# Two more groups of 256 tokens leave the attention rounds of a fused attention and MLP-mixer kernel for its late part

## The chip, the cores and the metric

The kernel runs on one core of a Trainium2 chip. The metric is the time of one execution on the device, in microseconds (us). The time is that of three runs: median, lowest and highest. Beside it stands one profiled execution, recorded by the hardware profiler, whose span runs from the first to the last instruction of the program. The engines are TensorE (PE in the profile, with its weight loads as PEld), VectorE (DVE), ScalarE (ACT), GpSimd (POOL) and SyncE (SP), which here only issues DMA transfers. A "q" behind an engine's name is the queue that issues its DMAs.

## What is computed

```python
# q, k, v: (8, 8, 576, 64) float32: batch, heads, tokens, head size
scores = (q @ k.transpose(0, 1, 3, 2)) / 8.0
thresh = scores.max(-1, keepdims=True) - tau            # tau = 0.02
scores = np.where(scores >= thresh, scores, -1e9)
attn = np.exp(scores - scores.max(-1, keepdims=True))
attn = attn / (attn.sum(-1, keepdims=True) + 1e-9)
x = (attn @ v).transpose(0, 2, 1, 3).reshape(8, 576, 512)

# w_tok1 (576, 256), w_tok2 (256, 576), w_ch1 (512, 1536), w_ch2 (1536, 512)
xt = x.transpose(0, 2, 1)
u = x + (np.maximum(xt @ w_tok1, 0) @ w_tok2).transpose(0, 2, 1)   # token MLP
out = u + np.maximum(u @ w_ch1, 0) @ w_ch2                         # channel MLP
```

Everything is float32; the MLP weights come as 64-bit numbers and are brought to float32 on the chip. A batch row has 576 tokens of 512 channels. The token MLP mixes all tokens of a row, so it can start when a row's attention is done. The channel MLP treats each token by itself, so it may be done for any group of tokens at any time after that.

## The kernel before, in words

**Attention.** The eight rows (here: batch entries, `b`) are worked one after the other. Two heads form a pair, two pairs a block of 1152 query rows, cut into nine units of 128. Two units are a *round*: 72 rounds in all, nine to a row, numbered here from 0, so that row 6 is rounds 54 to 62. A round's scores are products of TensorE (line 729) into a PSUM tile of its own pool. VectorE takes the maxima (742), GpSimd makes a bias of them (747), ScalarE masks (757) and exponentiates (767), VectorE inverts the sums (272, 273), GpSimd scales (280). Then the unit is turned: in row 0 by TensorE (295), in later rows by a VectorE transpose of 32 x 32 blocks (310) and four DMAs issued by SyncE (322, in the helper `move`). Three turned units make a group for the value products (360, 365), whose result is copied to `xT` (369), the row's activations with channels on partitions. There are two `xT` buffers, so row b + 2 writes the one that row b was in.

**Token MLP.** When a row's values are out, its token MLP follows: transposes (394), first layer (406), second layer (418), and an addition into `xT` by VectorE (428), so that `xT` now holds u.

**Channel MLP, now or late.** Of the 576 tokens of a row, `NOW[b]` groups of 256 (`GR`) get their channel MLP "now", by plain products placed between the rounds of the following rows: 12 steps of the first layer (834) with a relu each (ScalarE 839 or VectorE 842), and eight of the second layer (850), each added to the turned u by VectorE (864) and stored (874). The turn of u takes two VectorE transposes (819) and eight DMAs (826). In row 0 a group adds u by an identity product (848) instead and needs no turn. The tokens that are not done now are spilled to DRAM by one DMA a row (`spill`, 470). Row 7 has no groups now, and none of it is spilled.

**The late part.** After the last round the attention's memory is released and the remaining tokens are done in units of 512 (class `Late`): a channel MLP by Strassen's scheme with seven products of half-size blocks instead of eight, all on TensorE at line 1192. Its weight sums (`w1s`, `w2s`) are made by six VectorE operations, and sums of u (`t`) by four for each unit, at lines 1113 and 1116. The units are built from the list `put_off`, two groups of 256 each, and one more unit of the last 64 tokens of all rows. A unit's u is loaded from the spills (1147).

**What sets the order.** A planner written out in the kernel (class `Scheduler`) simulates the engines with given costs and emits instructions in the order that it finds; on the chip each engine then works strictly through its own list. All steps of TensorE outside the scores draw on banks of PSUM: two until the last round, four after it. Ranks decide between steps that are ready: value products 0, scores 1, token MLP 1.5, channel MLP 2. Besides, a round's scores are held back until the filling that has been done by the planner's count (`self.done`) has reached a due amount:

```python
total = sum(TOKENS + NOW[r] * GROUP for r in range(row))
part = TOKENS + NOW[row] * GROUP if row < B - 1 else 0.0
return total + part * (k - 2) / (UB // 2) - (KEEP_LAST if row == B - 2 else KEEP)
```

Here `row` is the row before the one whose rounds are placed, `k` the round in its row, `TOKENS` 18.8, `GROUP` 41.8, `KEEP` 14 and `KEEP_LAST` 20, in the planner's microseconds. A row's value products wait for the last reads of the `xT` two rows before it, the first layer of that row's groups and its spill among them.

Of the kernel before, what the change touches and what calls it, by code (L numbers as in the profile page):

```python
# [21 lines left out]
def kernel(  # L22
# [26 lines left out]
    B, H, S, D = q.shape  # L49
# [410 lines left out]
        return steps  # L460


    NOW = [2] + [1] * (B - 2) + [0]
    spilled = {}

    def spill(b):

        lo = GR * NOW[b]
        spilled[b] = dram.tile([P, NCC, S - lo], F32, name=f"spill_{b}")
# [335 lines left out]
    def make_groups(b, halves):  # L805
        uT = xTs[b]
        reads = []
        for i in range(NOW[b]):
            s = {}
# [240 lines left out]
    def planned_at(row, k):  # L1050
# [4 lines that stand above are left out]
# [72 lines left out]
    REST = S - 2 * GR  # L1127
    put_off = [(b, GR * i, GR) for b in range(B) for i in range(NOW[b], 2)]
    groups = [put_off[i : i + 2] for i in range(0, len(put_off), 2)]
    assert all(len(g) == 2 for g in groups) and not NOW[B - 1]  # L1130
    groups.append([(b, 2 * GR, REST) for b in range(B)])
# [239 lines left out]
```

## Time and profile before

| | us |
|---|---|
| median of three runs (lowest, highest) | 1346.2 (1345.57, 1347.57) |
| the profiled execution | 1346.21 |
| its span | 1344.3 |
| last round's scores begin | 895.7 |
| late part's first product begins | 976.5 |
| TensorE busy | 1261.7 |
| VectorE busy | 802.1 |
| ScalarE busy | 570.9 |

The profiled execution is 1.9 us longer than its span. A table of stretches is read so: first the stretch in us from the start of the span and its length, then for each engine the busy time and in brackets the number of instructions, then the clock that TensorE was granted (1.00 is full), the mean busy share of the 16 DMA engines and the rate at which they moved data. In a list of waits, three numbers stand behind a pair: us in total, how often, the longest. In a timeline the two leading numbers are the start and the length. A float32 product is recorded as two matmuls, so the first layer of a group has 96 records and the second 192.

### The profile page before, as it was taken

The page shows a single profiled execution, that of the slowest core. Times are in us where ns is not written, and L with a number is a line of the kernel's source. Part 1 is how long each engine was busy: PE and PEld are TensorE (multiplying, and loading weights), DVE is VectorE, ACT ScalarE, POOL GpSimd, SP SyncE. Part 2 cuts the span into 40 slices and gives each one's busy share as a digit, 9 for nine tenths or more (in the row PEclk, how much of TensorE's full clock was granted, in tenths as well). Part 3 has the DMA queues.
Part 4 walks back from the last instruction along what each step waited for, and adds up shares of the span by engine and source line. Part 5 has one row for each costly group of instructions (what it writes and reads, how often), then busy time and mean ns, then how long its engine had stood idle before and what let it go on. Part 6 is the DMA issues. An engine that isn't in the chain of part 4 may idle for free.

```text
span 1344.3 us, 21936 instructions
## 1 busy us (share of the span) xinstructions
PE 1261.7 (94%) x7982; PEld 1002.0 (75%) x7982; DVE 802.1 (60%) x1449; ACT 570.9 (42%) x1244; POOL 354.2 (26%) x658
## 2 busy tenths in 40 slices
PE   6778899999989999998999999899999999999998
PEld 5555579688657866875785776687988888888887
DVE  7899965384756766586576667665154443444352
ACT  6888654464644554455355537541020211112020
POOL 4666522142423323333233323320000000010100
PEclk7798899999989999999999999999999999999999
DMA  9655673463776575675667477173020211021011
GB/s 175 153 137 153 145 166 85 88 153 87 180 168 141 125 161 137 140 155 128 143 157 156 118 154 164 49 180 90 9 69 18 64 32 32 24 58 30 32 32 32
DMA packets 307194, 145.11 MB, mean 108 GB/s; under 512 B 206672, under 2 KB 299856, under 8 KB 307088
## 3 DMA queue, kind: packets, MB, share of 16 engines
q1 hardware_dynamic: 305216, 143.51, 46.3%
q8 instruction: 63, 1.03, 0.3%
q10 hardware_dynamic: 1872, 0.21, 0.1%
q14 instruction: 43, 0.35, 0.1%
HBM read 47.32 MB, written 13.50 MB: 45 GB/s over the span
## 4 chain that ended last, share of the span: by engine, by line
PE 58%; DVE 16%; SPq 10%; ACT 6%; DMA 6%; issue 3%; POOL 1%; DVEq 0%; ACTq 0%; POOLq 0%
PE o L1192 10%; PE bank L850 8%; PE bank L834 7%; SPq L322 6%; DVE mx L742 6%; PE hx L1192 6%; PE bank L365 5%; PE sc L729 5%; PE hz L1192 4%; PE oz L1192 4%; PE hmm L1192 4%; DVE T L310 3%; ACT e L757 3%; ACT e L767 2%; DMA eT<-T 2%
## 5 line engine op out<-in xcount | busy, mean ns | idle before, releaser
L757 ACT ACTIVATE e<-sc,bias 128x576 f32<-128x576 f32 x288 | 197.5, 741 | 223.6 <-DVE mx L742 180.8
L280 POOL TENSOR_SCALAR e<-e,rr 128x576 f32<-128x576 f32 x288 | 211.9, 750 | 284.9 <-DVE rr L273 239.1
L742 DVE TENSOR_REDUCE mx<-sc 128x1 f32<-128x576 f32 x288 | 198.1, 744 | 44.1 <-PE sc L729 44.1
L767 ACT ACTIVATE e<-e,ntau 128x576 f32<-128x576 f32 x288 | 221.0, 779 | 0.2
L310 DVE STREAM_TRANSPOSE T<-e 128x1152 f32<-128x1152 f32 x126 | 171.7, 1369 | 54.4 <-DMA eT<-T 42.3
L729 PE MATMUL sc<-kT,qT 64*128 64x192 f32 (+1 forms) x1920 | 176.4, 345 | 15.8 <-ACT e L757 13.6
L729 PEld LDWEIGHTS sc<-kT,qT 64*128 64x128 f32 (+1 forms) x1920 | 145.7, 183 | 47.9 <-issue 20.3
L850 PEld LDWEIGHTS bank<-wc,g 128*128 128x128 f32 x1536 | 175.0, 192 | 8.5 <-issue 4.9
L850 PE MATMUL bank<-wc,g 128*128 128x128 f32 x1536 | 180.0, 277 | 0.1
L834 PE MATMUL bank<-xT,wc 128*128 128x256 f32 x768 | 177.5, 384 | 0.9 <-DVE g L842 0.7
L834 PEld LDWEIGHTS bank<-xT,wc 128*128 128x128 f32 x768 | 142.4, 190 | 32.6 <-issue 7.5
L365 PE MATMUL bank<-eT,lv 128*64 128x384 f32 (+1 forms) x1024 | 146.5, 431 | 0.0
L747 POOL TENSOR_SCALAR bias<-mx,toff 128x1 f32<-128x1 f32 x288 | 77.7, 273 | 251.2 <-DVE mx L742 249.9
L1275 POOL TENSOR_TENSOR us<-us,ut 128x256 f32<-128x256 f32 x27 | 22.4, 844 | 393.2 <-DVE us L1113 393.2
L365 PEld LDWEIGHTS bank<-eT,lv 128*64 128x64 f32 x1024 | 81.8, 145 | 54.9 <-issue 38.6
L418 PE MATMUL bank<-w,a 128*128 128x288 f32 x256 | 72.4, 426 | 19.9 <-DVE xT L428 18.7
L272 DVE TENSOR_SCALAR rr<-rs 128x2 f32<-128x2 f32 x144 | 42.4, 294 | 68.0 <-ACT e L767 67.5
L418 PEld LDWEIGHTS bank<-w,a 128*128 128x128 f32 x256 | 47.0, 193 | 40.6 <-DVE xT L428 24.5
L406 PE MATMUL bank<-x_sb,w 128*128 128x512 f32 (+1 forms) x180 | 71.3, 549 | 0.6 <-DVE x_sb L398 0.5
L360 PE MATMUL bank<-eT,vl 128*64 128x384 f32 (+1 forms) x256 | 46.9, 444 | 20.1 <-DMA lq<-in_q_dram 3.8
L1240 ACT ACTIVATE ga<-hmm 128x256 f32<-128x256 f32 x30 | 11.5, 384 | 117.1 <-PE hmm L1192 117.1
L1113 DVE TENSOR_TENSOR temps<-hx,temps 128x256 f32<-128x256 f32 x60 | 25.1, 419 | 56.7 <-PE hx L1192 56.6
(128 smaller groups left out, 1552.4 us busy)
## 6 DMA issues: line engine op xcount, KB each, us to landing
eT<-T SPq DMA_DIRECT2D x504, 144.0 KB, 3.0
lk<-in_k_dram SPq DMA_DIRECT2D x126, 72.0 KB, 3.1
lq<-in_q_dram SPq DMA_DIRECT2D x124, 72.0 KB, 3.2
out_dram<-us SPq DMA_DIRECT2D x32, 256.0 KB, 2.1
ut<-us SPq DMA_DIRECT2D x128, 64.0 KB, 2.1
lv<-in_v_dram SPq DMA_DIRECT2D x112, 72.0 KB, 2.5
spare<-in_moe_w_ch_dram SPq DMA_DIRECT2D x8, 512.0 KB, 3.9
extra<-in_moe_w_ch_dram SPq DMA_DIRECT2D x8, 512.0 KB, 3.7
```

The source lines that it names most:

```text
L280: nc.gpsimd.tensor_scalar(out=eh, in0=eh, scalar1=rr[:, h : h + 1], scalar2=1.0, op0=ALU.mult, op1=ALU.mult)
L310: nc.vector.transpose(out=T.rearrange("p a (c x) -> p c a x", c=NK), in_=e.rearrange("p (c a x) -> p c a x", c=NK, a=4))
L322: nc.sync.dma_start(out=turned_e[key][:, place, i, :], in_=T[32 * i : 32 * i + 32])
L365: nc.tensor.matmul(to[r], lhsT=lv[:, j, :], rhs=e[j], start=False, stop=(c == NI - 1), skip_group_check=True)
L418: nc.tensor.matmul(bank[:, 0:HS], lhsT=hidden[b][:, m, P * c : P * c + P], rhs=w2[:, m, HS * f : HS * f + HS], start=(m == 0), stop=(m == ...
L729: nc.tensor.matmul(sc[h][rows, f, HT * k : HT * k + HT], lhsT=qT[r, cols], rhs=kT[r, HT * f : HT * f + HT], start=True, stop=True, skip_gr ...
L742: nc.vector.tensor_reduce(out=mx[:, h : h + 1], in_=part[h], axis=AX.XY, op=ALU.max)
L757: nc.scalar.activation(out=eh, in_=part[h], func=AF.Prelu, bias=bias[:, h : h + 1], scale=SCALE, alpha=STEEP)
L767: nc.scalar.activation(out=eh, in_=eh, func=AF.Exp, bias=ntau, accum_out=rs[:, h : h + 1])
L834: nc.tensor.matmul(bank[:, 0:n], lhsT=wc1[:, j, c, :], rhs=uT[:, c, GR * i : GR * i + n], start=(c == 0), stop=(c == NCC - 1))
L850: nc.tensor.matmul(to, lhsT=s["g"][:, j, P * t : P * t + P], rhs=wc2[:, j, P * c : P * c + P], start=(j == 0 and b > 0), stop=(j == NJ - 1 ...
L1192: nc.tensor.matmul(ps, lhsT=l, rhs=r, start=start and x == 0, stop=x == len(pairs) - 1, skip_group_check=not start)
```

## The change

One line of the kernel is different: the number of groups of each row that are done between rounds.

```diff
-    NOW = [2] + [1] * (B - 2) + [0]
+    NOW = [1, 1, 1, 1, 1, 0, 1, 0]
```

Before, the list is 2, 1, 1, 1, 1, 1, 1, 0: eight groups now. After, it has six: row 0 does one instead of two, row 5 none instead of one. The two groups go to `put_off`, which grows from eight groups to ten, and so from four late units of 512 tokens to five; the unit of the last 64 tokens of all rows stays. Row 0 spills 320 tokens instead of 64, row 5 all 576 instead of 320. The due amounts of the rounds follow `NOW`: rounds of row 1 count 60.6 of the planner's microseconds for row 0 instead of 102.4, and rounds of row 6 count 18.8 for row 5 instead of 60.6. The planner runs anew with all this, so that the order of instructions is different on every engine from round 14 on.

## The prediction

> **What bounds the kernel now.** I read the page first, then a table of busy time by stretches, cut where the rows of attention begin, then TensorE's waits, then its timeline.
>
> ```profile
> span 1344.3 us, 21936 instructions
> ...
> PE 1261.7 (94%) x7982; PEld 1002.0 (75%) x7982; DVE 802.1 (60%) x1449; ACT 570.9 (42%) x1244; POOL 354.2 (26%) x658
> ...
> PE 58%; DVE 16%; SPq 10%; ACT 6%; DMA 6%; issue 3%; POOL 1%; DVEq 0%; ACTq 0%; POOLq 0%
> ```
>
> TensorE (PE) is the busiest by far and leads the chain that ended last, but that chain also passes VectorE and the DMA issues of SyncE: the mean hides stages. The stretches, in order: the second half of row 1 (rounds 14 to 17), rows 2 to 7, the rest of the attention stage, and one late unit of 512 tokens.
>
> ```profile
> core 0: us, PE busy (x) PEld busy (x) DVE busy (x) ACT busy (x) POOL busy (x), PEclk, DMA share, GB/s
> 173.00:252.20 79.20, 78.61 (x566) 64.57 (x564) 33.76 (x60) 34.10 (x80) 18.84 (x36) 1.00 0.56 122
> 252.20:350.40 98.20, 95.69 (x689) 74.19 (x688) 64.04 (x112) 53.73 (x120) 32.87 (x68) 1.00 0.52 119
> 350.40:467.70 117.30, 107.65 (x785) 80.20 (x784) 75.83 (x138) 60.76 (x134) 35.80 (x72) 0.97 0.66 147
> 467.70:579.50 111.80, 105.08 (x754) 78.50 (x752) 74.07 (x135) 58.11 (x125) 36.06 (x73) 0.98 0.65 148
> 579.50:686.10 106.60, 100.83 (x714) 76.85 (x712) 70.80 (x131) 53.82 (x118) 35.38 (x72) 0.98 0.62 140
> 686.10:801.60 115.50, 107.84 (x785) 81.08 (x784) 77.76 (x143) 58.91 (x128) 37.95 (x75) 0.97 0.66 149
> 801.60:895.70 94.10, 88.06 (x602) 64.38 (x600) 63.53 (x114) 51.81 (x112) 32.53 (x66) 1.00 0.55 130
> 895.70:976.50 80.80, 80.80 (x542) 68.54 (x541) 29.23 (x44) 14.93 (x33) 3.99 (x8) 1.00 0.22 61
> 1049.00:1121.60 72.60, 72.60 (x338) 63.92 (x337) 31.33 (x58) 10.89 (x26) 4.91 (x6) 1.00 0.15 44
> ```
>
> The reader is to see that TensorE is never idle in the last two stretches, and idle 2 to 10 us in each row from 2 to 7; from row 1's second half to the last round that is 722.7 us elapsed less 683.8 busy, so 38.9 us. No other engine is above 68% there. So a microsecond of matmul taken out of the rows is a microsecond gained, as long as the rounds that are left still have enough matmuls to fill them. What idles TensorE in a row is seen in its waits and in one round:
>
> ```profile
> PE bank L418 <- DVE xT L428: 18.7, 12, 2.6
> PE sc L729 <- ACT e L757: 13.6, 6, 5.3
> ```
>
> ```profile
> 408.91 2.22 PE L729 MATMUL sc<-kT,qT 64*128 64x192 f32 x24
> 411.06 2.21 PE L418 MATMUL bank<-w,a 128*128 128x288 f32 x8
> 414.44 2.21 PE L418 MATMUL bank<-w,a 128*128 128x288 f32 x8 [1.18 <-DVE xT L428]
> 416.58 0.60 PE L729 MATMUL sc<-kT,qT 64*128 64x192 f32 x4
> ```
>
> Round 31 has nothing to offer TensorE between its scores and the next but a few products of the token MLP. These use the two PSUM banks that all filling shares, and VectorE, in its own order, empties them too late. Attention then sets the pace: from one score to the next 7.7 us, for 6.8 us of matmuls. I call a round lean if its matmuls are under 9.5 us.
>
> **The change part by part.** *What leaves the rows.* Two groups of 256 tokens: row 0's second and row 5's only one. Busy time of the first layer's line over row 0's second group, and of first and second layer over row 5's group:
>
> ```profile
> 204.60:320.80 116.20, 22.13 (x97) 17.75 (x96) 1.00 0.45 100
> ...
> 803.70:912.20 108.50, 22.11 (x96) 17.95 (x97) 1.00 0.55 131
> 803.70:912.20 108.50, 22.27 (x192) 21.69 (x192) 1.00 0.55 131
> ```
>
> Row 5: 22.1 + 22.3 = 44.4 us. Row 0: 22.1, half of the 44.73 us that line 850 has for both its groups, and half of 4.59 us for the identity products of line 848: 46.8. Together 91.2, the upper end. Where TensorE never stops, 56 first-layer records took 12.09 us (so 96 take 20.7) and 192 second-layer ones 21.44: two groups are 84.3, the lower end. Pricing each round of both programs by such durations (scores 2.25 or 3.4 us, 20 value records 3.0, a whole token MLP 21, and the rates above), the rounds 14 to 70 hold 706 us before and 639 after, and what follows the last round 85 and 66: 86.3 less. I take 87.5. Their relus, evacuations, the turn of row 5's tokens (two transposes of 1.13 us, eight DMA issues of 0.60 us on SyncE) and four stores go too, from engines and a queue with room, for nothing.
>
> *What comes.* A fifth late unit of 512 tokens with Strassen's seven products: 336 records, 72.5 us, as each of the four there (1013.1 to 1085.6 between like instructions). TensorE has no gap in them and VectorE, the next, is 31 us busy: +72.5 (to 72.6). Its load and stores ride on SyncE at a DMA share of 0.15.
>
> *What is less well filled.* By the order of instructions, rows 2 to 5 keep their filling (431 us after, 422 before), only shifted. Row 1's second half falls from 81 to 44 us, row 6 from 112 to 85, row 7 from 91 to 79. Before, 22 rounds from 14 to 70 are lean: 181 us of matmuls, 201.3 elapsed, so 9.15 us each. After, 23 are: 186 us, at 9.15 each 210.5, so 24.5 us of slack against 20.4: +4.0. Lower end: only what falls below 8.0 us, about the fastest lean round, is lost (8.4 against 6.5): +1.9. Upper: the seven lean rounds of rows 6 and 7 before took 9.4 each (7.5 us of slack); eight at that pace with 60.7 us of matmuls have 14.8: +7.3.
>
> *Rounds 14 to 17* were idle for 0.6 us in 79; at the 6 to 8% of rows 3 to 6, 44 us idle 3. They still have only first- and second-layer products and values to mix, and no tokens: +1 (0 to 3).
>
> *Spills.* Row 5 spills 1152 KB instead of 640, row 0 640 instead of 128. 640 KB landed in 4.1 us, 128 in 2.3, so each lands 1.8 us later. Queued behind them on SyncE are moves of turned scores (line 322), for which VectorE and the value products wait: +0.5 (0 to 3.6).
>
> *Clock.* Between 355 and 381 us TensorE was 20.84 us busy, with one wait of 3.83, and its granted clock was 0.87, so about 2.7 us were lost; in round 31, with a wait of 1.18, it was 1.00. A lean round is not paced by matmuls, so most of it is hidden: +0.5 (0 to 4, from one and a half such stretches).
>
> The Trainium skill ("TensorE: Matmul & The Clock Gate", Why this matters for your kernels) says that an idle gap beyond about 3 us between bursts sends the clock back to half. The 3.83 us wait with its 0.87 agrees. It speaks against this change, which thins the matmuls: were each of the eight lean rounds of rows 6 and 7 to lose half of a window of 3.4 us that the page states, an estimate from it is 8 x 1.7 = 13.6 us, and the sum would end near the time before. By the row I keep 0.5, since the longest of the twelve waits of line 418 is 2.6 us.
>
> *Row 7's values.* The xT buffers are two, so a row's first value product waits for the first-layer products two rows back; in rows 4 to 7 before, two value groups come at once after the last of these (rounds 40, 50, 59, 69). Row 5 has none after the change, and row 7's come in rounds 65 to 70 one or two at a time: -0.5 (-6, its whole idle time, to 0).
>
> *The end of the attention stage.* Before, six sums for the late part (10.5 us of VectorE, from 917.9 us) ran while 58 us of matmuls were left, and no evacuation stood among them. After, about 40 us are left there, second-layer products between the steps of row 7's tokens, and three of their evacuations stand on VectorE among the sums and the four that turn u into t, the first behind four sums, 7.0 us. After the attention stage there are four banks, not two, so TensorE can run ahead: +1 (0 to 7).
>
> *Sum.* -87.5 + 72.5 + 4.0 + 1 + 0.5 + 0.5 - 0.5 + 1 = -8.5 us. The profiled execution took 1346.21 us, span 1344.3 and 1.9 around it, and stands at the median of the three (1346.2). So 1337.7 us. All lower ends: 1323; all upper ends: 1359.
>
> **The rivals.**
> *More gain.* The matmuls were worth their busy time (-91.2) and row 7 loses its idle time (-6): 1346.2 - 8.5 - 3.7 - 5.5 = 1328.5. For it: row 7 becomes the smoothest row. Against: its idle time before has the token phase in it, which stays.
>
> *Nothing measurable.* VectorE's sums hold up the evacuations at the end (7, not 1) and row 1 takes its 3: 1337.7 + 8 = 1345.7. For it: VectorE works in its order, and a late transfer of u would hold all behind it. Against: four banks, and no wait at all there before.
>
> *Slower.* The rounds of rows 6 and 7 fall to the pace of the DMAs and of VectorE's order, in one place: the eight lean ones (54, 57, 58, 62, 64, 67, 68, 70). In each round SyncE issues eight moves and about five loads at 0.6 us, 8 us in all, and each round has 7.6 us of VectorE for attention alone (four maxima of 0.74, two transposes of 1.37, and smaller ones). The worst such round before:
>
> ```profile
> 613.00:625.00 12.00, 9.39 (x46) 6.59 (x44) 7.31 (x13) 6.25 (x13) 3.94 (x8) 0.86 0.88 206
> ```
>
> Here 7.9 us of work took 12 us, at a DMA share of 0.88. Eight at 12.0 instead of 9.15 are +22.8: 1360.5. It decides from 10.2 us a round, where the 8.5 are used up. Against it: most lean rounds took 7.5 to 10.
>
> That the change does not do what it says is excluded: the changed order has six groups in the rows and 2016 late matmul records instead of 1680.
>
> **How the numbers follow.** The forecast has 0.57, more gain 0.13, nothing measurable 0.12, slower 0.18. What this kernel's times can tell from no change is 0.2%, 2.7 us. Faster is 0.70, within 0.12, slower 0.18. The forecast's own range is 1331 to 1343; with the rivals 1328 to 1351, which leaves out the far half of the slower case and a little below.
>
> **What would show it.** Right: late matmuls begin near 895 us instead of 976.5, five units of 72.5 us follow, and TensorE's idle time from round 14 to the first late matmul is near 45 us instead of 39. Row 6 should take 90 us or less, row 7 near 85, their lean rounds about 9. Wrong: lean rounds of rows 6 and 7 above 10.2, a granted clock under 0.95 there, or a wait of TensorE on the second layer's evacuation after the last round.

## The result, and the profile after

The changed kernel takes 1341.5 us (median of 22 executions, 1335.5 to 1348.3) and the kernel before 1345.5 us (median of 22, 1341.2 to 1352.6) on the same chip. The ratio is 0.9970, with a 95% interval of 0.9956 to 0.9984: faster by 0.3%, about 4 us, where 8.5 us were forecast. On another chip the same two kernels stood at 1340.1 (12 executions) and 1342.0 (29): 0.9986, from 0.9971 to 1.0001. So the gain is real on the first chip, small, and at the edge of what can be told on the second.

The page of the changed kernel, the lines that answer to those shown of before:

```profile
span 1336.7 us, 21554 instructions
...
PE 1243.7 (93%) x7734; PEld 984.8 (74%) x7734; DVE 824.5 (62%) x1492; ACT 573.1 (43%) x1243; POOL 359.8 (27%) x664
...
PE 61%; DVE 13%; SPq 11%; DMA 7%; ACT 5%; issue 3%; POOL 1%; DVEq 0%; ACTq 0%; POOLq 0%
```

The stretches, cut at the same rounds as before: rounds 14 to 17, rows 2 to 7, the rest of the attention stage, and one late unit. Columns are start and end, length, busy time and instructions of each engine, granted clock, DMA share and rate.

```profile
173.40:219.50 46.10, 42.40 (x303) 33.04 (x301) 31.34 (x58) 26.23 (x59) 18.16 (x36) 1.00 0.81 177
219.50:317.00 97.50, 91.30 (x665) 68.29 (x663) 65.96 (x116) 56.88 (x125) 33.77 (x69) 0.98 0.61 140
317.00:430.70 113.70, 103.32 (x753) 78.97 (x752) 75.86 (x138) 57.12 (x124) 35.86 (x72) 1.00 0.65 147
430.70:540.00 109.30, 104.90 (x785) 79.40 (x784) 75.94 (x141) 58.91 (x128) 36.46 (x73) 1.00 0.67 150
540.00:661.80 121.80, 114.17 (x794) 87.00 (x792) 76.20 (x134) 60.23 (x132) 38.41 (x76) 0.97 0.63 144
661.80:747.80 86.00, 80.86 (x609) 59.54 (x608) 62.54 (x115) 54.62 (x115) 32.78 (x68) 1.00 0.70 158
747.80:835.00 87.20, 76.37 (x538) 51.65 (x536) 63.25 (x114) 49.41 (x107) 31.69 (x64) 0.96 0.66 156
835.00:896.50 61.50, 61.50 (x405) 50.20 (x405) 29.22 (x44) 14.20 (x33) 6.86 (x12) 1.00 0.27 70
...
896.50:969.00 72.50, 72.50 (x338) 63.65 (x337) 34.38 (x60) 10.88 (x26) 4.18 (x5) 1.00 0.15 44
```

The late part begins at 896.6 us instead of 976.5 and is one unit of 72.5 us longer. Rows 2 to 5 take about as long as before (442.3 us against 433.9), row 6 is down from 115.5 to 86.0, row 7 from 94.1 to 87.2, rounds 14 to 17 from 79.2 to 46.1. TensorE (the first busy column) is idle for 3.7 us in rounds 14 to 17 where it was 0.6, and for 10.8 in row 7 where it was 6.0.

A second profile of each kernel was taken (the first two experiments below, on two other chips), so the stages can be set beside each other twice, first pair and second pair, in us:

| | before | after | difference |
|---|---|---|---|
| up to round 14 | 173.1 / 174.1 | 173.5 / 172.4 | +0.4 / -1.7 |
| rounds 14 to 70, TensorE busy | 683.7 / 680.1 | 613.3 / 615.5 | -70.4 / -64.6 |
| rounds 14 to 70, TensorE idle | 38.9 / 38.6 | 48.3 / 47.3 | +9.4 / +8.7 |
| from the last round to the late part | 80.8 / 80.8 | 61.5 / 61.5 | -19.3 / -19.3 |
| late part | 362.9 / 362.9 | 435.4 / 435.4 | +72.5 / +72.5 |
| sum | | | -7.4 / -4.4 |

The spans differ by 7.6 and by 4.6 us; the rest lies behind the last product. So of the matmul time that the change saves, 17.2 us in the first pair and 11.4 in the second, some 9 go to rounds that TensorE no longer fills. Which executions are compared matters as much: the two pairs differ by 3 us, and both profiles of the changed kernel are of executions faster than its medians (1338.65 and 1338.69 us against 1341.5 and 1340.1).

### The profile page after: what moved, and what is told of

The parts are those of the page before. It is cut to its first block, busy times and chain, and to the rows that moved or that the text cites. A ratio compares the mean times of both kernels' runs of the same rounds, so it can differ in the third digit from the quotient of the medians.

```text
span 1336.7 us, 21554 instructions
## 1 busy us (share of the span) xinstructions
PE 1243.7 (93%) x7734; PEld 984.8 (74%) x7734; DVE 824.5 (62%) x1492; ACT 573.1 (43%) x1243; POOL 359.8 (27%) x664
## 3 DMA queue, kind: packets, MB, share of 16 engines
q1 hardware_dynamic: 307040, 146.13, 47.3%
## 4 chain that ended last, share of the span: by engine, by line
PE 61%; DVE 13%; SPq 11%; DMA 7%; ACT 5%; issue 3%; POOL 1%; DVEq 0%; ACTq 0%; POOLq 0%
PE o L1192 12%; PE hx L1192 7%; SPq L322 7%; PE sc L729 6%; PE bank L365 5%; DVE mx L742 5%; PE bank L850 5%; PE bank L834 5%; PE hz L1192 5%; PE oz L1192 5%; PE hmm L1192 5%; PE bank L418 2%; DVE T L310 2%; DMA eT<-T 2%; DMA lv<-in_v_dram 2%
## 5 line engine op out<-in xcount | busy, mean ns | idle before, releaser
L1275 POOL TENSOR_TENSOR us<-us,ut 128x256 f32<-128x256 f32 x33 | 27.3, 843 | 440.3 <-DVE us L1113 440.3
L365 PE MATMUL bank<-eT,lv 128*64 128x384 f32 (+1 forms) x1024 | 140.2, 416 | 0.0
L850 PEld LDWEIGHTS bank<-wc,g 128*128 128x128 f32 x1152 | 131.7, 192 | 7.2 <-issue 4.9
L850 PE MATMUL bank<-wc,g 128*128 128x128 f32 x1152 | 135.9, 277 | 0.1
L834 PE MATMUL bank<-xT,wc 128*128 128x256 f32 x576 | 134.5, 385 | 0.4 <-ACT x_sb L398 0.2
L834 PEld LDWEIGHTS bank<-xT,wc 128*128 128x128 f32 x576 | 106.4, 190 | 25.5 <-issue 5.4
L418 PE MATMUL bank<-w,a 128*128 128x288 f32 x256 | 75.1, 439 | 23.8 <-DVE xT L428 21.5
L272 DVE TENSOR_SCALAR rr<-rs 128x2 f32<-128x2 f32 x144 | 40.3, 280 | 61.2 <-ACT e L767 60.6
L1113 DVE TENSOR_TENSOR temps<-hx,temps 128x256 f32<-128x256 f32 x72 | 30.3, 421 | 68.4 <-PE hx L1192 68.3
```

The costliest lines, as they stand in the source:

```text
L365: nc.tensor.matmul(to[r], lhsT=lv[:, j, :], rhs=e[j], start=False, stop=(c == NI - 1), skip_group_check=True)
L418: nc.tensor.matmul(bank[:, 0:HS], lhsT=hidden[b][:, m, P * c : P * c + P], rhs=w2[:, m, HS * f : HS * f + HS], start=(m == 0), stop=(m == ...
L834: nc.tensor.matmul(bank[:, 0:n], lhsT=wc1[:, j, c, :], rhs=uT[:, c, GR * i : GR * i + n], start=(c == 0), stop=(c == NCC - 1))
L850: nc.tensor.matmul(to, lhsT=s["g"][:, j, P * t : P * t + P], rhs=wc2[:, j, P * c : P * c + P], start=(j == 0 and b > 0), stop=(j == NJ - 1 ...
```

## The experiments

The forecast rests on this theory, called A in most expectations: a stage lasts as long as its matmuls, except where a round has fewer of them than attention's own pace; what is lost there is slack. Its rivals: only the number of groups counts (D); TensorE bounds every round (B), or the other engines pace them all (R); and for the missing part of the gain, executions that differ among themselves.

**The same two kernels again.** First the changed kernel, with no edit.

> The changed kernel once more, unaltered. In its first profile the sum came out as worked out: rounds 14 to 70 took 61.1 us less than before, what follows the last round 19.3 less, the late part 72.6 more, 7.8 us in all; but the medians of many executions are only 4.0 us apart. Theory A (the executions of one kernel differ in the attention stage, by its waits and TensorE's granted clock, and the first profiles were a lucky pair): the second profile shows the late part at 72.5 us a unit and the end stage at 61 to 62 us as before, and rounds 14 to 70 longer than 661.6 us by about 3, with a clock of 0.97 or less. Theory B (the gain of the stages is real and 7.8): the second profile again has 661 to 662 us there, and the medians in this run are 7 to 8 apart.

Measured: 1340.1 us against 1342.0 before. The second profile has 662.8 us in rounds 14 to 70 and a clock of 0.975, nearly the first one's. So the changed kernel's first profile was no outlier among its profiles; but the medians are 1.9 apart, not 7 or 8, so this expectation's B falls too. That left the profile of before, taken again, also unaltered.

> The kernel before once more, for a second profile. The first had 722.6 us from round 14 to the last round, 38.9 of them idle for TensorE, and a granted clock of 0.975 over the span; other executions of this kernel have a mean clock of 0.977. Theory A (the first profile of before was a slow draw, and so the gain of 7.6 us between the first profiles is too large): the second has a higher clock, a shorter stage, 717 to 720 us, with the end stage and the late part unchanged at 80.8 and 362.9. Theory B (it was typical): 722 to 723 again.

Measured: span 1341.5, rounds 14 to 70 in 718.7 us, clock 0.976. Theory A of this run holds: the first profile of before was about 3 us slower than the second. The difference lies in matmuls that took longer at a lower clock, not in waits: idle time is 38.9 and 38.6, busy time 683.7 and 680.1. The same stretch of 115.5 us, row 6 in the first profile and some 3 us more than row 6 in the second, holds 785 matmul records at a granted clock of 0.97 and 805 at 0.99:

```profile
686.10:801.60 115.50, 107.84 (x785) 81.08 (x784) 77.76 (x143) 58.91 (x128) 37.95 (x75) 0.97 0.66 149
```

```profile
686.10:801.60 115.50, 108.94 (x805) 83.09 (x802) 80.09 (x146) 58.26 (x127) 39.02 (x76) 0.99 0.67 152
```

In the first profile two short stretches of this row have half the clock. TensorE had just waited 2.0 us in front of the one and 2.3 us in front of the other:

```profile
706.10:709.30 3.20, 3.20 (x12) 1.49 (x10) 0.42 (x1) 3.20 (x8) 0.26 (x1) 0.50 0.87 220
781.20:784.40 3.20, 3.20 (x12) 1.50 (x10) 0.00 (x0) 3.20 (x9) 0.00 (x0) 0.50 0.93 234
```

The second profile has one such stretch in row 6. In rounds 14 to 70 the clock is at half for 20 us in the first profile and for 14 in the second.

**Which rows give up their groups.** Six groups again, with row 6's put off instead of row 5's:

```diff
-    NOW = [1, 1, 1, 1, 1, 0, 1, 0]
+    NOW = [1, 1, 1, 1, 1, 1, 0, 0]
```

> Six groups between the rounds as in the change, but row 6 gives up its group and row 5 keeps it. Pricing the rounds by the order of instructions: rounds 9 to 70 hold 23 us more matmuls than in the change, what follows the last round 23 us less, and the slack of lean rounds is 3.5 us smaller. Theory A (which row gives up its group matters only through slack and the end): 1338 us, the same as the change within 4. Theory C (the end stage needs filling that covers the six weight sums on VectorE, 10.5 us, and the token steps of row 7): the end stage has only 43 us of matmuls and shows 8 to 14 us of idle TensorE, 1346 to 1352.

Measured: 1339.4 us, ratio to before 0.9978 (0.9963 to 0.9994), within 1 us of the changed kernel on that chip. The end stage, now 44.1 us, has 3.4 us of idle TensorE, not 8 to 14: the weight sums need little cover, and C falls. Then both groups from row 0:

```diff
-    NOW = [1, 1, 1, 1, 1, 0, 1, 0]
+    NOW = [0, 1, 1, 1, 1, 1, 1, 0]
```

> Both of row 0's groups wait for the late part, row 5 keeps its group: again six groups. Rounds 14 to 17 have hardly any filling. Theory A (a group taken from rounds that stay filled is gained, one taken from rounds that fall under the pace of attention, about 8.6 us a round, is lost in slack): the slack of lean rounds is 38 us instead of 20, matmuls of the attention stage are the same within 2 us: 17 us slower than the change, 1357. Theory D (what counts is only the number of groups and Strassen's saving): 1340, the same as the change within 4.

Measured: 1346.4 us, ratio 1.0025 (1.0009 to 1.0042): slower than before, and 6 us slower than the changed kernel. That is between A and D: idle time of TensorE in rounds 14 to 70 is 52.7 us, only 4.4 over the changed kernel's; rounds 14 to 17 and row 2 have 16 us more of it, later rows less. The direction is A's, the size a third of it. In the profiles 7 us more come from matmuls that are longer busy (681.9 against 674.8 us from round 14 to the late part), which A does not have. And four groups:

```diff
-    NOW = [1, 1, 1, 1, 1, 0, 1, 0]
+    NOW = [1, 0, 1, 0, 1, 0, 1, 0]
```

> Four groups between the rounds (rows 0, 2, 4 and 6), four more than before in the late part, which gets a sixth unit of 512 tokens. Theory A: matmuls fall by another 85 us and the late part grows by 72.5, but slack of lean rounds grows from 20 to 46 us: 14 us slower than the change, 1354. Theory D (each pair of groups saves what the first saved): 1337 or less. The floor of a round, 8.6 us in this sum, is read from the rounds without filling.

Measured: 1359.6 us, ratio 1.0135 (1.0107 to 1.0162). D falls: the second pair costs 19 us where the first gained 2 to 4. A's 1354 is 5 too low. TensorE idles 65.1 us in rounds 14 to 70.

**No group at all,** to see the pace of attention with the token MLP alone.

```diff
-    NOW = [1, 1, 1, 1, 1, 0, 1, 0]
+    NOW = [0] * B
```

> No group between the rounds at all, all 4608 tokens in the late part: nine units and none of the first- and second-layer products at lines 834 and 850. It measures the pace that attention keeps with the token MLP alone as filling (rounds of 4 to 12 us of matmuls). Theory A (a floor of 8.6 us a round, as in the lean rounds before): rounds 9 to 70 take 580 us, the total is 59 us above the change, 1398. If the floor is 8.0 the total is 1370 to 1375, if 9.2 about 1420. The granted clock falls under 0.96 if it follows TensorE's idle time.

Measured: 1429.1 us (one execution), with nine late units in 652.8. Rounds 9 to 70 take 605 us where a floor of 8.6 gave 580, and rounds 14 to 70 take 9.66 us each. So the mean pace was set too low. It is no floor of a single round: in the changed kernel rounds 57, 58 and 62 took 7.6 to 7.7 us. That such rounds are short because matmuls were waiting from the round before is likely and not shown. TensorE's waits in rounds 14 to 70, and that stretch:

```profile
PE sc L729 <- ACT e L757: 52.7, 32, 5.3
PE bank L360 <- DMA eT<-T: 23.2, 10, 4.0
PE bank L418 <- DVE xT L428: 19.0, 10, 4.2
```

```profile
170.60:721.40 550.80, 434.96 (x2972) 281.75 (x2968) 418.93 (x752) 345.12 (x738) 225.51 (x455) 0.89 0.77 174
```

No engine is over 80% busy, not even TensorE. The scores wait for ScalarE's mask, that is for the score buffers of the round before, the values for the moves of turned scores, and the token MLP for VectorE: by these waits a loop through the engines sets the pace, not the work of one of them.

**Matmuls left out, the order kept.** One edit, made in both kernels; all other instructions keep their place.

```diff
-                for j in range(NJ):
+                for j in range(0, NJ, 2):
                     nc.tensor.matmul(
                         to,
...
-                        stop=(j == NJ - 1),
+                        stop=(j == NJ - 2),
```

In the kernel before:

> The kernel before with every second product of the channel MLP's second layer left out in the groups between the rounds, all else in place and in order: about 86 us fewer matmuls, 70 of them in the rounds and 16 after the last. Theory A (a round lasts as long as its matmuls, but not under about 8.6 us): 72 us less. Theory B (TensorE bounds every round): 86 less. Theory R (attention's other engines pace the rounds): 16 to 25 less.

In the changed kernel:

> The same omission in the changed kernel: 64 us fewer matmuls, 53.5 in the rounds and 10.7 after the last. Theory A: 48 us less, a smaller share than in the kernel before, because more rounds are already lean. Theory B: 64 less. Theory R: 11 to 18 less.

Measured, in two executions each: 1329.7 against 1343.1 in the kernel before, 13 us less (ratio 0.9896, 0.9841 to 0.9951), and 1323.3 in the changed kernel (1319.4 and 1327.3), 17 to 18 below its medians on other chips. Theories A and B fall, and badly: of 86 and 64 us of matmuls only a sixth and a quarter come back. R is nearest: it gave 16 to 25, which is a little too much, and 11 to 18. Rounds 14 to 70 of the changed kernel, whole and with the omission:

```profile
173.40:835.00 661.60, 613.31 (x4438) 457.89 (x4436) 451.09 (x813) 363.39 (x787) 227.13 (x456) 0.99 0.66 150
```

```profile
172.30:825.40 653.10, 573.84 (x3960) 411.04 (x3960) 449.33 (x814) 363.14 (x787) 227.00 (x456) 0.97 0.67 152
```

The 478 records that are missing are worth 53 us (at 21.44 us for 192), TensorE is busy for 39.5 us less, and the stretch is 8.5 shorter. Some 14 us go to the matmuls that are left, which take longer; the clock is at half for 37 us of this stretch, for 17 without the omission. The other 31 are more idle time. A good part of it is at the value products, which TensorE reaches earlier: its waits at line 360 in this stretch, as far as the profile lists them, grow from 23.7 to 41.6 us, and most of them end with a DMA. So with the order kept, fewer matmuls gain little, while the change, which takes 65 to 70 us of them out there and lets the planner place the rounds anew, shortens the same stretch by 56 to 61. Attention's own pace alone is not what holds it, since the kernel without groups does these rounds in 550.8 us. A reading that fits is that the planner spaces all engines' lists to fit TensorE's, and then none has room to be faster; so 93% of busy TensorE does not mean that TensorE bounds each round. It is argued and not shown: the change also takes some 8 us of work each from VectorE and ScalarE in this stretch, which the omission leaves there, and what part of the gap each list holds was not separated.

**One wait in row 7.** In the two profiles of the changed kernel TensorE waits 6.4 and 6.6 us in round 64, at row 6's last group of value products. The timeline there of TensorE, VectorE and SyncE (start, length, what):

```profile
758.97 2.94 PE L850 MATMUL bank<-wc,g 128*128 128x128 f32 x24
768.28 1.55 PE L360 MATMUL bank<-eT,vl 128*64 128x384 f32 x4 [6.36 <-DMA out_dram<-us]
```

```profile
753.15 2.63 DVE L310 STREAM_TRANSPOSE T<-e 128x1152 f32<-128x1152 f32 x2
```

```profile
752.13 0.65 SPq L106 DMA_DIRECT2D lq<-in_q_dram  x1
...
756.60 0.50 SPq L106 DMA_DIRECT2D lq<-in_q_dram  x1
757.14 0.50 SPq L106 DMA_DIRECT2D lk<-in_k_dram  x1
757.74 2.63 SPq L120 DMA_DIRECT2D lv<-in_v_dram  x4
760.47 5.11 SPq L322 DMA_DIRECT2D eT<-T  x8
```

VectorE has turned both units by 755.8 us. Their eight moves stand in SyncE's list behind eight loads of queries and keys and four of values for a pair that begins only three rounds later, and so go out from 760.5 on. (The store that the profile names as the end of the wait is issued right behind these moves.) The edit: in the planner, that pair's loads come after the moves of row 6's last two units.

```diff
-                        after=(key_op("load", n - 1, LOADS - 2),),
+                        after=(key_op("load", n - 1, LOADS - 2), key_op("M", 2 * last_round(n - 2) - 5) if n == 4 * B - 2 else None),
...
-            put(("loadv", n), sched.op("sp", 2.0, lambda: load_v(n), (free,), 0, after=(key_op("loadv", n - 1),), dmas=(4, 70, 0.5) if n >= NP else (1, 280, 0.5)))
+            put(("loadv", n), sched.op("sp", 2.0, lambda: load_v(n), (free,), 0, after=(key_op("loadv", n - 1), key_op("M", 2 * last_round(n - 2) - 5) if n == 4 * B - 2 else None), dmas=(4, 70, 0.5) if n >= NP else (1, 280, 0.5)))
```

> The changed kernel with one thing moved on SyncE: the eight loads of queries and keys and four of values of row 7's third pair are issued behind the eight moves of row 6's last two units, not ahead of them. Up to round 62 the order of instructions is the same. In the two profiles of the changed kernel a value product of round 64 waits 6.4 and 6.6 us there, while the moves, whose data is ready at 755.8 us, are issued from 760.5 on behind the loads. Theory A (SyncE's order makes this wait): the wait falls to 2 us or less, rounds 63 to 70 have 4 to 6 us less idle TensorE (10.8 before), and the total is 3 to 5 us under the change. Theory B (the row is paced by VectorE and ScalarE anyway): the wait is gone, idle time shows up in other rounds, and the total is the same within 2.

Measured: 1334.4 us against 1344.7 before, ratio 0.9926 (0.9913 to 0.9940): faster than both kernels (the changed one had 0.9970 and 0.9986 on other chips). SyncE and TensorE at the same place:

```profile
754.35 5.11 SPq L322 DMA_DIRECT2D eT<-T  x8
759.51 0.60 SPq L106 DMA_DIRECT2D lq<-in_q_dram  x1
```

```profile
762.75 0.87 PE L360 MATMUL bank<-eT,vl 128*64 128x384 f32 x4 [1.04 <-DMA lk<-in_k_dram]
```

The wait is down to 1.0 us. Round 64, from one round's scores to the next, with the same 69 matmul records in both, in the changed kernel and with the edit:

```profile
756.30:773.90 17.60, 11.24 (x69) 7.21 (x68) 10.03 (x20) 9.14 (x21) 6.91 (x12) 0.81 0.79 181
```

```profile
755.90:766.10 10.20, 9.01 (x69) 6.56 (x68) 6.80 (x15) 9.33 (x22) 4.89 (x10) 1.00 0.87 176
```

The round is 7.4 us shorter: 5.2 less idle time, and 2.2 less busy, at a clock of 1.00 instead of 0.81. TensorE's list is the same up to round 66; from there the planner laid out the rest anew, and 2 to 3 us are lost again. The idle time of rounds 63 to 70 is down from 10.8 to 7.4, a little less than the 4 to 6 us that A expected, and the late part begins at 891.5 us, 5.1 earlier. The rest of A holds: SyncE's order made the wait. The same rule for all pairs of rows 2 to 7, here for the loads of queries and keys, and in the same way for the values:

```diff
-                        after=(key_op("load", n - 1, LOADS - 2), key_op("M", 2 * last_round(n - 2) - 5) if n == 4 * B - 2 else None),
+                        after=(key_op("load", n - 1, LOADS - 2), key_op("M", 2 * last_round(n - 2) - 5) if n >= 2 * NP else None),
```

> The same rule for every pair of rows 2 to 7: its loads go behind the moves of the units that are turned when it becomes possible to load. Theory A: every row has some of this wait (28.5 us of VectorE's time and 10.7 of TensorE's waits are put down to moves), and the total is 5 to 10 us under the change. Theory B: the loads, now later, are waited for instead, and the total is the same within 4.

Measured: 1355.0 us, ratio 1.0080 (1.0063 to 1.0096), 20 us worse than the single place. TensorE idles 57.5 us in rounds 14 to 70, and one wait of a value product, which the profile puts down to a load, is 8.6 us long. Neither theory gave such a loss; that the loads are now late is likely, as B has it, and not shown further. With row 6's list on top:

```diff
-    NOW = [1, 1, 1, 1, 1, 0, 1, 0]
+    NOW = [1, 1, 1, 1, 1, 1, 0, 0]
```

> Rows 6 and 7 without groups, row 5 with one, and the loads behind the moves: the two edits that may beat both kernels, together. If the gain of the loads' order adds to that of row 6's list: 1333 to 1337. If the two meet the same wait: 1338 to 1341.

Measured: 1350.9 us, ratio 1.0046 (1.0032 to 1.0061): the general rule costs here too, and neither of the two expectations came.

**The spills.**

```diff
         nc.sync.dma_start(out=spilled[b], in_=xTs[b][:, :, lo:])
+        again = dram.tile([P, NCC, S - lo], F32, name=f"again_{b}")
+        nc.sync.dma_start(out=again, in_=xTs[b][:, :, lo:])
```

> The changed kernel with each row's spill written twice, the second time to a place that nobody reads: 4992 KB more of DMA and seven more issues on SyncE, where the change itself spills 1024 KB more than before. It measures the price of a spill. Theory A (the forecast's 0.5 us for 1024 KB): 2 to 3 us over the change. The upper bound of the forecast, 3.6 us for 1024 KB, would make 17 us. If spills are hidden altogether: within 1.5 of the change.

Measured: 1339.1 us, against 1344.7 of the kernel before on that chip, ratio 0.9951 (0.9930 to 0.9971), and 1340.1 and 1341.5 of the changed kernel on others. Five times the change's own extra spill costs nothing that can be seen, as far as a comparison across chips can tell. The upper bound of the forecast, 17 us, is out: the spills are hidden.

## Why the prediction was right, and where it was not

It was right in direction, and 1341.5 lies in its range of 1328 to 1351; the likeliest value, 1337.7, was 4 us too low, and the gain twice too large. The mechanism held: two groups' matmuls leave, a unit of Strassen's scheme comes, and idle time in the rounds takes most of the difference. That the first pair of profiles, with 7.6 us, comes so near to 8.5 is in part luck: more matmul time left than was forecast, which hid some of the larger slack. Of the named signs of being right, row 6 (86.0 us), row 7 (87.2) and the late part's start came true. Two of the named signs of being wrong showed in row 7: round 64 took 17.6 us, and the granted clock of the row was 0.96 in the first profile and 0.94 in the second, with 0.95 as the mark.

- *What leaves the rows* was put at 87.5 us (84.3 to 91.2). The two pairs of profiles give 89.7 and 83.9, about 1 less on average, and the larger one owes some 3 us to the slower clock in the first profile of before.
- *What comes* was exact: 72.5 us, without a gap.
- *The slack* is the term that was mis-sized. All terms beside what leaves and what comes were +6.5 us together; measured are 9.4 and 8.7, all in the rounds. By place, first pair and second: rounds 14 to 17 +3.1 and +3.5 (forecast +1, at most 3), rows 2 to 5 +4.0 and +1.8, row 6 -2.5 and -1.6, row 7 +4.8 and +5.0. So the idle time did not grow where rounds are leanest: row 6, which lost most of its filling, came out with less of it than before.
- *Row 7* is where the sum lacked a term. The -0.5 for row 7's own values was about right: none of them waits, and without round 64 the row has 4.5 us of idle time where it had 6.0. But in round 64 the last value products of row 6 wait 6.4 us for moves that stand behind SyncE's loads, and for this the sum had nothing. The slower rival had named this queue with its eight moves and five loads a round. It happened in one round of the eight that it named: they took 9.2, 7.6, 7.6, 7.7, 17.6, 8.5, 10.2 and 9.4 us, 9.7 on average and 8.6 without round 64, where the forecast had 9.15 and the rival 12.0. Moving the loads took the wait away and about 5 us with it, about as much as the forecast had too much. It is not the whole account: the first pair of profiles has this wait too and comes within 1 us of the forecast gain, so that the rest differs from one execution to the next.
- *Spills* (+0.5) and *the end of the attention stage* (+1) cost nothing: no idle time is found after the last round, and spilling twice changed nothing.
- *Clock*, +0.5 (0 to 4), was too low for the typical execution, as far as can be told. Its reason, that no wait of line 418 is longer than 2.6 us, does not carry: in the kernel before, half the clock followed waits of 2.0, 2.0, 2.3 and 2.6 us too, and in the changed kernel that line has waits of 4.3 and 4.5. The mean granted clock of many executions is 0.977 before (29, 9 and 11 executions on three chips, 0.9769 to 0.9775) and 0.973 after (22 and 12, 0.9728 and 0.9733), while the first profiles both had 0.975. Over the 22 executions after, time and clock go together: 1348.3 us at 0.968, 1335.5 at 0.977, 1.2 us for each 0.001 (correlation -0.82). On the second chip it is 0.7 for each 0.001; in 11 executions of the kernel before on a third it is 0.2 (correlation -0.37), and in the ten of the run with row 6's list put off none. So 0.004 would answer to 5 us at the most, perhaps to much less, where 3.6 are missing between the first profiles' 7.6 and the first chip's 4.0. Whether the clock makes the time or longer waits make both was not separated.

The rule of the Trainium skill ("TensorE: Matmul & The Clock Gate", Why this matters for your kernels), that a gap beyond about 3 us lowers the clock, agrees with row 7: a stretch of 13 us around the wait of 6.4 has 0.89, and 6.7 us behind the wait have 0.50. As a threshold it does not fit this case, where waits of 2.0 to 2.6 us were followed by half the clock as well, though not each of them. The estimate from that page, 13.6 us for eight lean rounds, was too high: of the eight only round 64 lost clock in the first profile, 2.2 us.

```profile
756.00:769.00 13.00, 6.64 (x56) 5.51 (x56) 6.74 (x15) 8.35 (x19) 4.00 (x8) 0.89 0.73 166
766.10:772.80 6.70, 4.52 (x15) 1.93 (x17) 4.87 (x9) 3.99 (x10) 4.38 (x6) 0.50 0.83 205
```

- *The sentence that a microsecond of matmul taken out of the rows is a microsecond gained* had a condition, that the rounds left still have enough matmuls to fill them, and this was not enough. It nearly held for the change (61 and 56 us gained for 70 and 65 less busy), where the planner laid out the rounds again. With the order kept, 8.5 us came back for 39.5 less busy, in rounds that were 93% busy before.

## What to carry to other kernels

A busy share of 93% does not say that an engine bounds the time, least of all where a planner has spaced all lists to fit it: take some of its work out with the order kept, and see how much comes back. Before moving work from a mixed stage into a cheaper one, price the stage that is left by its own pace, measured with the work gone, not by its fastest rounds. And look at the order of the queue that only issues DMAs: eight transfers behind twelve that nobody needed yet cost as much as the whole change gained.

## What the runs showed that was not expected

The mean granted clock falls as TensorE's idle time in rounds 14 to 70 grows: 0.977 with 39 us idle (eight groups), 0.973 with 48 (the changed kernel), 0.971 with 53 (row 0 without groups), 0.969 with 58 (all loads behind the moves), 0.963 with 65 (four groups) and 0.935 with 116 (none, one execution). Half the clock can follow a wait as short as 2.0 us, and two profiles of one kernel, with the same order of instructions, differ by 3 us, about what 7 us more at half the clock can cost. Attention with the token MLP alone keeps to 9.66 us a round with no engine above 80%. And issuing loads later is worth 5 us at one place, and costs 9 to 15 when it is made a rule (by the ratios to before, against the same lists without the rule).
